# Who issues the DMAs: loads, rows of maxima and stores given to Sync, ScalarE or GpSimd by a new written order

## The chip, the cores and the metric

The kernel runs on one core of a Trainium2 chip. A core has five engines with a queue of instructions each: TensorE (PE, with its weight loads as PEld), VectorE (DVE), ScalarE (ACT), GpSimd (POOL) and Sync (SP). Each works through its own queue in order, and an instruction that waits holds all that stand behind it on that engine. The core's 16 DMA engines move data between memory and the on-chip buffer; a DMA is started by an instruction in the queue of Sync, ScalarE or GpSimd. The metric is the device time of the whole program in microseconds.

## What is computed

Two stages run one after the other: a linear attention with exponential features over 64 heads (8 batches of 8), 576 positions and 64 channels, and a feed-forward layer with a maximum of three products over its 4608 rows of 512.

```python
def phi(x):
    proj = np.einsum('bhsd,df->bhsf', x, w_phi)
    proj = proj - np.max(np.abs(proj), axis=-1, keepdims=True)
    return np.concatenate([np.exp(proj), np.exp(-proj)], axis=-1)
q_p, k_p = (phi(q), phi(k))
kv = np.einsum('bhsf,bhsd->bhfd', k_p, v)
z = np.sum(k_p, axis=2)
num = np.einsum('bhsf,bhfd->bhsd', q_p, kv)
den = np.einsum('bhsf,bhf->bhs', q_p, z)[..., None] + 1e-06
attn = num / den
...
x = np.ascontiguousarray(attn.transpose(0, 2, 1, 3)).reshape(B * S, H * D)
h = np.maximum(np.maximum(x @ w1, x @ w2), x @ w3)
out = h @ w_out
```

The inputs and the output are in float32; the products are made in bfloat16 with float32 sums.

## The kernel before

**Units and chunks.** The attention is cut into 16 units of four heads (two pairs), two units for each batch. A unit loads q, k and v as 128 rows of 18 tiles (576 KB each in float32), has them cast to bfloat16 (units 0 to 3: by the DMA or on ScalarE and VectorE; later ones on GpSimd, L480) and turned (units 0 to 3 on TensorE, L494 and L497; later ones by a transposing DMA from Sync, L512, into qkT). Then TensorE projects every tile (L535, in groups of four or two tiles, on halves of 64 rows), VectorE takes the largest absolute value of each row (L554) and ScalarE the two exponentials of k (L548). The maxima of q are turned on TensorE, copied out (L566, tile mT), and written by a small DMA, the "row of maxima", as one more row of qkT (L570), so that the product for q (L614) subtracts them; ScalarE then makes its exponentials (L627). The maxima of k become factors em (L585), by which GpSimd scales v (L589, tile vab, with a column of its own from L599). TensorE sums over the positions (L643, kvps), multiplies with q's exponentials (L661, psn), VectorE divides (L667, L668), and x is turned into xT (units 0 and 1 on TensorE, L681; later ones by a transposing DMA from Sync, L691).

The feed-forward layer works in 9 chunks of 512 positions, one for each batch, and a last one for the 64 remaining positions of all batches. A chunk makes six tiles of up-products in two rounds (L714, ups), evicted by ScalarE or VectorE (L722, L724: first round; L720: second round), then four tiles of output (L741 and L746, ops), evicted by ScalarE or VectorE (L754, tile osb, four buffers) and stored (L761, two DMAs for a tile; one in the last chunk, whose last tile is cut into three pieces). Weights are loaded by casting DMAs from GpSimd (L421); differences of them are made by six subtractions (L784, on VectorE or GpSimd; after one on VectorE, GpSimd makes a small copy at L787), and a product of the first table with w_out (L812, pm, evicted at L816) at the start.

**The written order.** Every piece of work is a Node with a table of costs, whose keys are the engines that it may run on, and a function that issues its instructions. The string PLAN (L96 to L245) lists all 1478 nodes in order. An entry is the node's number, a letter for its engine (T, D, A, G, S for TensorE, VectorE, ScalarE, GpSimd, Sync), a digit for the slot of each buffer that this node is the first to use, and the start that was planned for it. `plan` (L251) sets engine, start and slots from it; `fill` (L269) puts products with no use into gaps of TensorE's plan near the start (L843, `idler`, to keep its clock up), and issues all in the order of the planned starts. So the table fixes the order of each engine's queue, who does a piece of work that several engines may do, and which buffers are shared; the planned starts are not waited for. The nodes speak of "mode" for TensorE's use of 64 rows (1: L535 and L643; 2: L497) or of all 128 (0).

Loads come through L474 (the four first halves of unit 0 through L449; those of units 1 to 3 for q and k, which are cast on the way, from GpSimd through L463). A load needs its raw buffer free: there are two each for q and k, four for v. Three loads of v wait in addition for a tiny copy on VectorE (L472), which sets when they start. `queue_of` (L336) maps an engine's name to its queue; stores, rows of maxima and, after the change, loads use it.

Of the kernel before, what the change touches and what calls it, by code (L numbers as in the profile page):

```python
# [15 lines left out]
B, H, S, D = 8, 8, 576, 64  # L16
# [15 lines left out]
FULL = 1.45  # L32
# [64 lines left out]
0G@0.70 2D0@0.70 4A@0.70 10S0@0.70 3D@0.90 6S0@1.18 1G@1.25 8S@1.66 86G0@1.75 13S@2.14 85G@2.60 15S0@2.62 1076G@3.45 12A1@3.98  # L97
158G2@4.25 7D@4.96 159G@5.10 5D@5.46 16T1@5.61 9A@5.94 1079G@5.95 17D0@6.30 22T002300@7.08 27T45@7.30 26D@7.55 30D@8.15 14A@8.43
25D@8.76 23A@9.05 20T6@9.20 18T7@9.31 31D@9.37 21D@9.97 227G1@10.01 28A@10.12 19D@10.20 42T14@10.35 29A@10.62 45D@10.81
32T26@10.96 24A@11.11 46D@11.15 37T75@11.26 35D@11.49 34A@11.60 89T1@11.60 91T3@12.04 47A0@12.09 40D@12.10 44A@12.34 48G0@12.48  # L100
39A@12.68 90D1@12.71 61T20@12.86 33A@13.16 64T7@13.31 92D@13.33 228G@13.60 38A@13.65 36D@13.95 95T111311@14.10 66A@14.14
49G@14.45 41D@14.56 65A@14.63 43A@15.12 99D@15.16 110T67@15.27 63A@15.46 50G@15.57 55T5@15.61 98D@15.77 1077G@15.85 111A@15.94
1090T4@16.06 113D@16.38 62A@16.43 1088T1@16.66 56A@16.91 114D@16.98 67T2@17.26 97A@17.40 1086T6@17.49 1089D0@17.59 51A@17.89
69A@18.14 87D1@18.21 53G@18.29 58T0@18.34 1087D@18.34 88S@18.46 68A@18.48 57A@18.82 164T1@18.89 361S1@18.94 1091D@18.96
59A@19.30 93T2@19.34 52G@19.41 162T6@19.45 165D2@19.59 112A@19.79 166T5@19.90 163D@20.21 60A@20.28 105T41@20.36 54G@20.52
1078G@20.80 106A@20.83 108D@20.83 70T070@20.95 96A@21.32 160D2@21.44 167D@21.54 161S@21.69 94D@21.76 109D@21.98 100T64@22.05
296S0@22.17 115T53@22.27 101A@22.52 72D@22.59 362S1@22.65 1094T2@22.75 119D@22.96 102A@23.02 117A@23.50 104D@23.66 116A@23.84
1096T0@24.05 107A@24.18 103D@24.26 124A1@24.68 118D@24.87 120A@24.93 127G1@25.07 71A@25.18 1095D@25.21 183T003400@25.44
1097A@25.59 173T16@25.66 168T57@25.88 123A@26.09 177D@26.13 1098T2@26.23 185A@26.24 170A@26.73 186D@26.74 125G@27.00 175A@27.22
176D@27.35 137T01@27.52 184A@27.71 171D@27.95 77T30@27.98 126G@28.12 138A@28.23 1092T1@28.29 78D0@28.56 139A@28.71 172D@29.18  # L110
1099A@29.20 122G@29.23 79T5@29.58 174A@29.70 187D@29.79 75T3@29.90 1093A@30.18 140T0@30.21 121G@30.35 229D3@30.39 131T2@30.44
76D1@30.50 141A@30.69 73T6@30.89 142A@31.03 80D0@31.11 128T4@31.21 132A@31.37 11G@31.47 364G0@31.62 74D1@31.73 178T13@31.76
133A@31.85 143T105@31.98 130A@32.34 181D@32.35 129A@32.82 182D@32.96 188T26@33.08 233T1@33.31 145A@33.33 192D@33.57 144A@33.73
134T4@33.88 191D@33.91 196A0@34.13 234D0@34.25 146T51@34.34 190A@34.38 198G0@34.53 148T0@34.65 135A@34.72 147D0@34.90
235T2@35.06 231T1@35.17 189A@35.20 149D1@35.52 199A@35.55 136A@35.70 152T5@35.74 193T6@36.05 232D@36.14 179A@36.18 81T0@36.29
83T4@36.60 197G@36.62 169A@36.67 153D0@36.76 150T1@36.91 194A0@37.16 154T7@37.31 236D@37.38 180A@37.41 195S@37.56 151D1@37.60
242T115611@37.72 84A@37.90 247T23@38.05 155D@38.22 297S0@38.34 156T1@38.39 82D@38.69 230S@38.82 215T047@38.87 157A@38.95
1080D@39.16 426S1@39.30 249A@39.60 1081D@39.78 1104T0@40.09 244A@40.09 1082D@40.40 248A@40.58 1106T1@40.95 250D@41.02 216A@41.07
365G@41.37 251D@41.63 1102T4@41.81 1107A1@42.06 246D@42.23 1105A@42.56 366S1@42.64 1110T2@42.67 245D@42.84 243A@43.06
1084D@43.45 1108T3@43.54 1103A@43.55 1111A@44.05 1085D@44.07 252T10@44.50 217A@44.55 1083D@44.69 257T56@44.72 237T42@44.83  # L120
1109A@44.95 1112T7@45.17 240D@45.31 259A@45.45 299G2@45.66 239A@45.79 255D@45.91 1124T3@46.04 254A@46.28 1113D@46.52 253A@46.77
1422G@46.78 1116T4@46.90 260D@47.13 300G@47.18 238A@47.26 1125D@47.47 556S0@47.65 258A@47.75 209T10@47.76 262T7@47.98
1118T5@48.04 241D@48.09 263A1@48.29 429G1@48.30 211A@48.54 264S@48.69 261D@48.70 212T3@48.90 203T7@49.01 210A@49.02 1117D@49.04
1120T2@49.23 363S0@49.47 204A@49.51 1119D@49.66 427S1@49.95 205A@49.99 200T6@50.09 256D@50.28 1122T1@50.30 214A@50.48
1121D@50.89 265A1@51.04 206T4@51.17 213A@51.29 266G1@51.44 367T005700@51.48 1123D@51.51 202A@51.63 301S2@51.63 382T02@51.70
1114T3@52.04 201A@52.11 386D@52.17 370D@52.78 1130T1@52.91 384A@52.93 1115D@53.39 208A@53.42 267G@53.53 224T60@53.77 207A@53.91
371D@54.01 220T5@54.08 383A@54.39 275T31@54.40 1131T@54.61 385D@54.62 369A@54.88 225D0@55.22 368A@55.37 1101G@55.62 221D1@55.84
276A@55.86 222T4@55.90 491S1@56.07 218T2@56.22 1132A0@56.35 223D0@56.47 272T0@56.53 278T6@56.74 268G@56.82 273A@56.99
372T75@57.06 219D1@57.09 430G@57.10 284T114@57.28 277A@57.48 376D@57.70 226S@57.85 274A@57.96 375D@58.31 377T23@58.38 280A@58.45
1126T0@58.72 286D@58.92 279A@58.93 380D@59.30 373A@59.42 281T7@59.58 387T46@59.79 285D@59.91 282A@59.94 269T2@60.06 1127T@60.27  # L130
283A@60.28 381D@60.29 431S0@60.52 271A@60.62 391D@60.89 270A@61.11 390D@61.23 293T11@61.56 395A0@61.59 374A@61.84 291T7@61.87
396G0@61.99 294D0@62.12 289T4@62.19 379A@62.33 1134T2@62.50 290D1@62.75 1128A1@62.82 287T5@63.36 292D0@63.37 388A@63.43
1138T1@63.68 378A@63.77 288D1@63.99 397G@64.08 389A@64.26 317T114011@64.64 295S@64.76 302T73@64.86 312T65@65.08 319A@65.11
320D@65.11 1135T@65.42 313A@65.60 321D@65.75 303A@66.09 559G0@66.18 316D@66.35 304A@66.58 1139T@66.71 557S0@66.88 305D@66.96
1136A2@67.07 398G@67.30 298S1@67.36 306D@67.57 1100G@67.58 314A@67.68 392T4@68.00 307T72@68.16 318A@68.17 315D@68.17
414T053@68.38 308A@68.66 1140D3@68.78 309A@69.15 393D0@69.40 322T06@69.48 310D@69.60 1142T1@69.71 394S@69.75 323A@69.84
324A@70.18 311D@70.21 416A@70.52 622S1@70.53 1154T4@70.57 560G@70.68 325D@70.82 1143A0@70.92 1129S@71.01 326D@71.16 415A@71.42
1146T7@71.44 1155D@71.69 751S0@72.21 327T2@72.30 447T003000@72.45 328A1@72.61 432T16@72.68 1137S@72.69 442T54@72.90 448A@72.93
450D@72.93 1144T2@73.24 443A@73.42 445D@73.53 428S2@73.89 1147A@73.91 1152T3@74.10 451D@74.14 1141S@74.37 434A@74.41 1145D@74.75
444A@74.90 402T50@74.97 1148T7@75.18 435D@75.36 403A@75.43 818S3@75.57 330A1@75.92 411T2@76.05 329S@76.05 1150T1@76.16  # L140
404A@76.17 1149D@76.30 331G1@76.32 492S0@76.83 436D@76.91 1162T5@77.02 1151A@77.27 623S0@77.31 1153A@77.77 408T7@77.88
1156T1@78.10 1163D@78.13 412A@78.27 333G@78.41 413A@78.61 332G@78.69 446D@78.75 433A@78.95 1164T3@78.96 1157D@79.36 409A@79.44
405T5@79.82 449A@79.92 1158T2@80.04 1165D@80.07 406A@80.41 494G2@80.78 399T4@80.90 1160T6@81.12 1159D@81.15 401A@81.37
561S1@81.37 407A@81.85 437T10@82.08 1161D@82.23 349T132@82.30 400A@82.34 410A@82.82 441D@82.85 495G@83.27 452T54@83.40
1174T6@83.63 350A@83.65 455D@83.76 438A@84.05 351D@84.10 625G1@84.39 440D@84.48 340T71@84.49 439A@84.54 343T3@84.71 337T5@84.93
453A@85.03 334T2@85.14 421T00@85.36 344A@85.37 346T1@85.67 1175T@85.78 342A@85.85 422D0@85.92 496S2@86.20 336A@86.34 456D@86.54
345A@86.82 1166T0@87.07 348A@87.31 1176D1@87.32 347A@87.65 423T3@87.93 460A0@87.99 338A@88.24 419T6@88.25 462G0@88.39
424D1@88.50 417T1@88.56 335A@88.72 1167T@88.87 420D0@89.12 341A@89.21 339A@89.69 418D1@89.74 352T31@90.16 1168A2@90.41
354T2@90.47 754G0@90.48 425S@90.51 457T7@90.79 356T6@90.85 454A@91.02 355D0@91.04 358T5@91.16 458A0@91.36 577T111011@91.57
461G@91.60 353D1@91.66 572T47@91.79 1170T2@92.13 574A@92.26 359D0@92.28 579A@92.75 357D1@92.90 1171T@93.00 573A@93.24 575D@93.52  # L150
# [143 lines left out]
def kernel(  # L294
# [577 lines left out]
```

## Time and profile before

| what | value |
|---|---|
| median of 3 runs | 284.23 us (283.29 to 285.58) |
| profiled execution, span from first to last instruction | 282.5 us |
| 284.23 less the span | 1.7 us |
| busy share of PE, DVE, ACT, POOL | 96%, 75%, 68%, 40% |
| bytes read and written | 34.64 MB, 9.44 MB |
| granted clock of TensorE | 1.00 until the end |

The profile is taken from one execution. Its page gives only the span, no time of that execution measured from outside; the 1.7 us between span and median is what lies around it, start and last landing among them. In the views below, "SPq", "ACTq" and "POOLq" are the parts of an engine that wait and issue; a line such as "PE pm L812 <- DMA wout_bf: 1.0, 1, 1.0" tells who waited for whom, with the total in us, the number of waits and the longest. A row of groups gives line, engine, operation, output and input, the count, then busy us and mean ns, then the idle time just before and what ended it. In the view of the chain that ended last, a row is start, length and what it was.

### The profile page before, as it was taken

To read this page: it belongs to the slowest core of one execution; us is meant where nothing else is said; L and a number is where in the kernel's file an instruction comes from. 1 tells how busy PE (TensorE), PEld (TensorE's weight loads), DVE (VectorE), ACT (ScalarE), POOL (GpSimd) and SP (SyncE) were. 2 spreads that over 40 slices of the span, in tenths; PEclk is the share of its full clock that TensorE was granted. 3 is DMA by queue.
4 is the path that set the end of the run, shared out by engine and by line. 5 is a ranking of instruction groups with operands and counts; after the bars stand their busy time and mean duration, and the time that the engine had idled before them with its cause. 6 is when DMAs were issued, how large, how long until landed. Compare 5 with 4: busy or idle time off the path is not lost.

```text
span 282.5 us, 8556 instructions
## 1 busy us (share of the span) xinstructions
PE 271.2 (96%) x3521; PEld 154.0 (54%) x3560; DVE 211.6 (75%) x443; ACT 192.3 (68%) x449; POOL 113.2 (40%) x106
## 2 busy tenths in 40 slices
PE   8888979999999999999999999999999999999995
PEld 3565764566555644764556456555455465444443
DVE  4998989998877888679989876997477594254141
ACT  2897979898889779998585879977707961311111
POOL 8373567748176418913760563053033600000000
PEclk9999999999999999999999999999999999999999
DMA  7999999888999999999797866954975105600154
GB/s 202 240 206 282 280 273 240 266 204 167 300 363 198 175 308 300 194 165 277 212 199 129 246 235 124 166 102 167 186 177 116 40 4 104 137 2 0 37 123 139
DMA packets 68337, 51.45 MB, mean 182 GB/s; under 512 B 48778, under 2 KB 53066, under 8 KB 68298
## 3 DMA queue, kind: packets, MB, share of 16 engines
q1 hardware_dynamic: 63876, 45.74, 66.8%
q0 software_dynamic: 4000, 4.92, 10.0%
q8 instruction: 28, 0.46, 0.7%
q10 hardware_dynamic: 422, 0.24, 0.3%
q14 instruction: 11, 0.09, 0.1%
HBM read 34.64 MB, written 9.44 MB: 156 GB/s over the span
## 4 chain that ended last, share of the span: by engine, by line
PE 80%; DMA 11%; DVE 4%; issue 2%; SPq 1%; DVEq 0%
PE ups L714 31%; PE ops L746 14%; PE ops L741 10%; DMA wout_bf<-in_moe_w_out_dram 6%; PE psn L661 6%; PE kvps L643 5%; PE psm L614 5%; PE psq L535 4%; PE pm L812 2%; DMA out_dram<-osb 2%; DMA xT<-x_sb 2%; DVE x_sb L668 2%; DMA k_raw<-in_k_dram 1%; DVE mqp L554 1%; DVE mk L554 1%
## 5 line engine op out<-in xcount | busy, mean ns | idle before, releaser
L714 PE MATMUL ups<-xT,w_bf 128*128 128x512 bf16 x416 | 100.3, 379 | 1.4 <-DMA xT<-x_sb 0.3
L589 POOL TENSOR_TENSOR vab<-v_raw,em 128x1152 bf16<-128x1152 f32 (+1 forms) x36 | 68.2, 1907 | 67.2 <-ACT em L585 50.9
L548 ACT ACTIVATE Ek<-psk 128x512 bf16<-128x512 f32 (+1 forms) x160 | 80.8, 569 | 13.9 <-PE psk L535 10.1
L627 ACT ACTIVATE Eq<-psm 128x512 bf16<-128x512 f32 (+1 forms) x160 | 79.2, 570 | 7.3 <-PE psm L614 7.0
L714 PEld LDWEIGHTS <-w_bf 128*128 128x128 bf16 x432 | 41.0, 98 | 47.4 <-issue 0.4
L554 DVE TENSOR_REDUCE mqp<-psq 128x4 bf16<-128x512 f32 (+1 forms) x80 | 48.8, 631 | 6.3 <-PE psk L535 4.4
L746 PE MATMUL ops<-wout_bf,hT 128*128 128x512 bf16 (+2 forms) x215 | 49.3, 367 | 1.0 <-issue 0.5
L554 DVE TENSOR_REDUCE mk<-psk 128x4 f32<-128x512 f32 (+1 forms) x80 | 48.5, 628 | 2.4 <-PE psk L535 1.7
L720 DVE TENSOR_TENSOR hT<-hT,ups 128x512 bf16<-128x512 bf16 x54 | 36.1, 682 | 16.4 <-PE ups L714 12.7
L668 DVE TENSOR_TENSOR x_sb<-psn,rden 128x320 bf16<-128x320 f32 x64 | 31.5, 492 | 2.2
L746 PEld LDWEIGHTS <-hT 128*128 128x128 bf16 x228 | 21.1, 98 | 21.7
L722 ACT ACTIVATE hT<-ups 128x512 bf16<-128x512 f32 x33 | 19.1, 603 | 17.3 <-PE ups L714 15.8
L661 PEld LDWEIGHTS <-Eq 128*128 128x128 bf16 x640 | 25.0, 97 | 7.8 <-ACT Eq L627 0.2
L754 DVE COPY osb<-ops 128x512 f32<-128x512 f32 (+1 forms) x22 | 14.7, 669 | 16.8 <-PE ops L746 16.0
L661 PE MATMUL psn<-kv_sb,Eq 128*128 128x65 bf16 x640 | 26.9, 194 | 0.2 <-DVE mqp L554 0.2
L754 ACT COPY osb<-ops 128x512 f32<-128x512 f32 (+2 forms) x16 | 8.9, 562 | 23.2 <-PE ops L746 22.6
L741 PE MATMUL ops<-xT 128*128 128x512 bf16 x90 | 24.1, 380 | 0.3
L535 PE MATMUL psq<-w,qkT 64*128 64x128 bf16 x288 | 24.3, 217 | 0.1
L535 PE MATMUL psk<-w,qkT 64*128 64x128 bf16 x288 | 24.0, 217 | 0.4 <-ACT Eq L627 0.4
L535 PEld LDWEIGHTS <-qkT 64*128 64x128 bf16 x576 | 16.5, 94 | 12.0 <-issue 8.9
L614 PE MATMUL psm<-qkT,wphi_m 128*128 128x512 bf16 (+1 forms) x70 | 22.1, 358 | 0.0
L480 POOL CAST qk_bf<-q_raw 128x1152 bf16<-128x1152 f32 x12 | 13.8, 1147 | 20.3 <-DMA out_dram<-osb 9.4
(73 smaller groups left out, 230.9 us busy)
## 6 DMA issues: line engine op xcount, KB each, us to landing
v_raw<-in_v_dram SPq DMA_DIRECT2D x16, 576.0 KB
out_dram<-osb SPq DMA_DIRECT2D x64, 128.0 KB
q_raw<-in_q_dram SPq DMA_DIRECT2D x12, 576.0 KB
k_raw<-in_k_dram SPq DMA_DIRECT2D x12, 576.0 KB
w_bf<-in_moe_w_dram POOLq DMA_DIRECT2D x3, 768.0 KB, 20.3
qk_bf<-in_k_dram POOLq DMA_DIRECT2D x3, 288.0 KB, 13.9
qk_bf<-in_q_dram POOLq DMA_DIRECT2D x3, 288.0 KB, 13.4
wout_bf<-in_moe_w_out_dram POOLq DMA_DIRECT2D x1, 768.0 KB, 17.7
```

The source lines that it names most:

```text
L535: nc.tensor.matmul(ps()[:, i, :], lhsT=cols[r, :], rhs=w2[r, c, :], start=True, stop=True)
L548: nc.scalar.activation(Ek[s]()[:, tiles_of(t0, n), :], of(1), EXP, scale=1.0 - 2.0 * s)
L554: nc.vector.tensor_reduce((mq, mk)[c]()[:, tiles_of(t0, n)], of(c), AXX, ALU.max, apply_absolute_value=True)
L589: (nc.vector if n_.eng == "DVE" else nc.gpsimd).tensor_tensor(vab()[:, g, t0:t1, 0:D], vb()[:, t0:t1, :], em()[:, g, t0:t1].unsqueeze(2).t ...
L614: nc.tensor.matmul(psm()[:, 0:w], lhsT=wphi_m, rhs=rhs, start=True, stop=True)
L627: nc.scalar.activation(Eqb()[s][:, cols], psm()[:, 0:w], EXP, scale=1.0 - 2.0 * s)
L661: nc.tensor.matmul(psn()[:, c, :], lhsT=Eqb()[g][:, t0:t0 + P], rhs=kv()[:, pr, ab, g, :], start=(g == 0), stop=(g == 1))
L668: nc.vector.tensor_tensor(x_sb()[:, pr, :, ab, :], psn()[:, :, 0:D], rden().to_broadcast([P, 5, D]), ALU.mult)
L714: nc.tensor.matmul(ups(), lhsT=w_bf[i + 1][:, ct, j * P:(j + 1) * P], rhs=tokens_of(ct), start=(ct == 0), stop=(ct == CT - 1))
L720: nc.vector.tensor_tensor(hT()[:, j, :], hT()[:, j, :], ups(), ALU.max)
L741: nc.tensor.matmul(ops_()[:, 0:width], lhsT=tile_of(ct, tt), rhs=line_w[c_i > MOVE][:, ct, cols], start=(ct == 0), stop=False)
L746: nc.tensor.matmul(ops_()[:, 0:width], lhsT=hT()[:, j, tt * P:(tt + 1) * P], rhs=wout_bf[:, j, cols], start=False, stop=(j == JT - 1))
```

## The change

The edits of code are small: `queue_of` knows GpSimd; a load through L474 goes to the queue of its node's engine; and loads, rows of maxima and stores list the engines that may issue them. The table is new as a whole, 1478 entries again. It gives the same pieces of work another order on all engines, other slots, and for those that may run on several engines another choice. For the loads through L474 (40, all Sync's before) it names Sync 19 times, GpSimd 14 and ScalarE 7 times; for the 14 rows of maxima Sync 9, GpSimd 3 and ScalarE 2 times (before: Sync 12, ScalarE 2); for the 38 store steps Sync 20, GpSimd 14 and ScalarE 4 times (before: Sync 36, ScalarE 2). Of the six subtractions at L784 four go to GpSimd (before: all VectorE). Copies and evictions that VectorE, ScalarE or GpSimd may do also change sides in both directions.

```diff
-0G@0.70 2D0@0.70 4A@0.70 10S0@0.70 3D@0.90 6S0@1.18 1G@1.25 8S@1.66 86G0@1.75 13S@2.14 85G@2.60 15S0@2.62 1076G@3.45 12A1@3.98
...
+0G@0.72 6S0@0.73 2D0@0.85 3D@1.07 10S0@1.19 1G@1.29 4A@1.30 8S@1.65 85G0@1.79 13S@2.11 86G@2.64 1076G@3.49 7A1@3.63 15G0@4.29
+12D@4.68 158G2@5.14 16T1@5.33 9A@5.42 5D@5.85 159G@5.99 17D0@6.55 1079G@6.84 22T002300@7.32 27T45@7.56 25D@7.81 30D@8.41
...
-    queue_of = {"SP": nc.sync, "ACT": nc.scalar}
+    queue_of = {"SP": nc.sync, "ACT": nc.scalar, "POOL": nc.gpsimd}
...
-                mains.append(nd("Lv" if what == 2 else "L", {"SP": 0.62}, lambda what=what, raw=raw: nc.sync.dma_start(
-                    by_pairs(raw()), rows_of(what, u, 0, 2)), gates, [raw],
-                    pipe=(EARLY if u == 0 or u == BY_PE and what == 1 else 1.0) * FULL, hold=-3.0, lat=1.7,
-                    packet=PACKET))
+                def main(n_, what=what, raw=raw):
+                    queue_of[n_.eng].dma_start(by_pairs(raw()), rows_of(what, u, 0, 2))
+                n_ = nd("Lv" if what == 2 else "L", {"SP": 0.46, "ACT": 0.5, "POOL": 0.85}, None, gates, [raw],
+                        pipe=(EARLY if u == 0 or u == BY_PE and what == 1 else 1.0) * FULL, hold=-3.0, lat=1.7,
+                        packet=PACKET)
+                n_.fn = lambda n_=n_, f=main: f(n_)
+                mains.append(n_)
...
-            n_v = nd("V", {"ACT": 0.7, "SP": 0.7}, None, [n_mt] + projs, [mT, qkT], lat=2.2, pipe=0.1)
+            n_v = nd("V", {"ACT": 0.7, "SP": 0.7, "POOL": 0.9}, None, [n_mt] + projs, [mT, qkT], lat=2.2, pipe=0.1)
...
-                n_ = ff("store", {"SP": 0.6 * n_out, "ACT": 0.6 * n_out} if c_i == B else {"SP": 0.6 * n_out}, None, [e], [part],
+                n_ = ff("store", {"SP": 0.6 * n_out, "ACT": 0.6 * n_out, "POOL": 0.9 * n_out}, None, [e], [part],
```

Entry 15, for one, is the load of v of unit 0: 15S0 before, 15G0 after. In the changed file the lines behind L474 stand 3 lower.

More of the change, by code (lines that the diff above doesn't have):

```diff
@@ L101 @@
[L101 to L131, printed above, removed]
@@ L245 @@
+1465G@277.44 1474T5@277.83 1475T@278.05 1468A0@278.08 1469S@278.60 1476A2@278.63 1477A@278.90
 """
```

261 lines of the change are left out of this document (145 added, 116 removed).

## The prediction

> **What bounds the kernel now.** I read the page first, then the busy time by stages, then TensorE's own list of waits, and only then the list of the Sync queue, because the change is about issuing.
>
> ```profile
> span 282.5 us, 8556 instructions
> PE 271.2 (96%) x3521; PEld 154.0 (54%) x3560; DVE 211.6 (75%) x443; ACT 192.3 (68%) x449; POOL 113.2 (40%) x106
> ```
>
> ```profile
> 0.00:10.00 10.00, 8.43 (x54) 3.84 (x55) 5.78 (x19) 3.79 (x5) 5.87 (x13) 1.00 0.86 224
> 10.00:50.00 40.00, 36.33 (x719) 24.84 (x721) 36.87 (x80) 35.14 (x88) 24.26 (x30) 1.00 1.11 250
> 50.00:250.00 200.00, 197.34 (x2603) 111.05 (x2634) 158.29 (x330) 148.71 (x348) 83.03 (x64) 1.00 0.80 185
> ```
>
> The columns after the length are the busy time of TensorE (PE), its weight loads, VectorE, ScalarE and GpSimd, then the granted clock (1.00 throughout), the busy share of the DMA engines and GB/s. TensorE is the bound: between 50 and 250 us it is busy 197.34 of 200 us, so only 2.66 us are free there. Between 10 and 50 us 3.67 us are free, and in that stage the DMA engines are full (share 1.11). These 6.3 us are all that better issuing can give back. Next, who makes TensorE wait:
>
> ```profile
> PE pxT L681 <- issue: 1.3, 1, 1.3
> PE pm L812 <- DMA wout_bf<-in_moe_w_out_dram: 1.0, 1, 1.0
> PE ups L714 <- DMA xT<-x_sb: 0.3, 1, 0.3
> PE tps L497 <- DMA qk_bf<-in_q_dram: 0.3, 1, 0.3
> PE tps L497 <- DMA qk_bf<-in_k_dram: 0.3, 1, 0.3
> ```
>
> Waits that end with a transfer come to 1.0 + 0.3 + 0.3 + 0.3 = 1.9 us; one pause of 1.3 us has no releaser. The Sync queue tells another story:
>
> ```profile
> SPq L761 <- ACT osb L754: 21.3, 3, 19.3
> SPq L570 <- ACT Ek L548: 16.5, 3, 15.2
> SPq L474 <- DVE v_raw L472: 15.2, 1, 15.2
> SPq L761 <- DVE osb L754: 12.9, 9, 2.8
> ```
>
> Sync stands for tens of us behind evictions and gates, and the loads and transposes of the same queue stand behind it. But nearly none of it arrives at TensorE: the loads were issued early enough. That is the first reason for my forecast.
>
> **The change part by part.** Counted over both tables: of the 40 loads through L474 that Sync issued alone in the old table, the new one gives 14 to GpSimd and 7 to ScalarE; of the 14 rows of maxima 3 to GpSimd, and 2 are on ScalarE as before; of the 38 store steps 14 to GpSimd (12 of two DMAs, 2 of one, so 26 DMAs) and 4 to ScalarE (2 before). GpSimd gets 14 + 3 + 26 = 43 more DMAs. The same table also reorders every engine: four of the six subtractions of weight tables (L784) go from VectorE to GpSimd, and evictions change sides.
>
> *GpSimd's 43 DMAs.*
>
> ```profile
> L463 POOL DMA_DIRECT2D qk_bf<-in_k_dram x3 | 2.5, 817 | 0.0
> L463 POOL DMA_DIRECT2D qk_bf<-in_q_dram x3 | 2.2, 719 | 4.1 <-issue 4.1
> L421 POOL DMA_DIRECT2D w_bf<-in_moe_w_dram x3 | 2.4, 803 | 0.0
> L784 DVE TENSOR_TENSOR w_bf<-w_bf 128x1024 bf16<-128x1024 bf16 x6 | 3.8, 680 | 0.0
> L819 POOL COPY w_bf<-xT 128x1024 bf16<-128x1024 bf16 x2 | 2.1, 1042 | 0.0
> L589 POOL TENSOR_TENSOR vab<-v_raw,em 128x1152 bf16<-128x1152 f32 (+1 forms) x36 | 68.2, 1907 | 67.2 <-ACT em L585 50.9 <-DMA v_raw<-in_v_dram 13.7 <-issue 2.5
> L480 POOL CAST qk_bf<-k_raw 128x1152 bf16<-128x1152 f32 x12 | 13.7, 1148 | 13.8 <-DMA k_raw<-in_k_dram 13.8
> ...
> L589 POOL TENSOR_TENSOR vab<-v_raw,em x36: 1144/2123/2131, 12.4 to 223.6; 128x1152 bf16<-128x1152 f32 x28, 128x576 bf16<-128x576 f32 x8
> ...
> POOL vab L589 <- ACT em L585: 50.9, 11, 14.1
> ```
>
> A GpSimd issue keeps the engine for (2.5 + 2.2 + 2.4) / 9 = 0.79 us, whatever the size. A store or a row of maxima from GpSimd is not in the trace; between the 0.35 us of a store from ScalarE (below) and the 0.82 us here I take 0.79, the same engine. 43 x 0.79 = 34 us. A subtraction on GpSimd is not there either; it lies between the 1.04 us of a copy of that size and the 2.12 us of a full L589 product (its median), and I take the product: 4 x 2.1 = 8 us. GpSimd goes from 113 to about 155 us of 282. What hides it are its own waits, 67.2 us ahead of L589, of which 50.9 us in 11 waits for ScalarE's em (the last row: total, number, longest). The fullest stretch that I find in the new order is from about 96 to 124 us: 4 full products (8.5), 5 casts at 1.15 (5.7) and 9 DMAs (7.1) make 21.3 of 28 us. It fits, so I take 0. If the cover is gone, L589 is late, then the sums kvps (L643) on TensorE; that is a rival below, with +5.7 as the upper end.
>
> *Queues moved past.* Sync loses these issues, ScalarE gains 7 loads and two more store steps.
>
> ```profile
> L474 SPq DMA_DIRECT2D v_raw<-in_v_dram x16: 368/512/662, 2.6 to 205.2; - x16
> L761 SPq DMA_DIRECT2D out_dram<-osb x68: 332/587/1353, 72.7 to 279.7; - x68
> L761 ACTq DMA_DIRECT2D out_dram<-osb x2: 338/348/357, 278.0 to 279.2; - x2
> L570 ACTq DMA_DIRECT2D qkT<-mT x2: 717/1020/1324, 153.8 to 191.0; - x2
> ```
>
> The figures are shortest/median/longest in ns. Seven loads at the 0.51 us that Sync takes are 3.6 us of ScalarE, 68% busy before; queued behind each stand one or two exponentials (L548, L627), for which TensorE waits next. Bounds 0 (hidden) and +3.6 (all on the path); since ScalarE's busy time from 50 to 250 us leaves 51 us, I take 0. Sync's relief acts on the 2.66 us that TensorE is idle from 50 to 250 us. One such chain is visible:
>
> ```profile
> 97.94 5.07 DMA out_dram<-osb
> ...
> 103.10 0.69 DVE osb L754
> ...
> 107.43 1.02 PE ups L714 x4
> ```
>
> A store lands 5.07 us after its issue, in the middle of loads of the same queue; VectorE's next eviction waits for its buffer, and up-products follow. Bounds -2.7 (all of it goes) and 0; I take -0.6, less than a quarter, because most of the 2.66 us are short and spread, with no row above that names a transfer.
>
> *The start.* v of unit 0 goes from Sync to GpSimd's queue, ahead of two loads of unit 2 and of wout. Its 576 KB at the stage's 250 GB/s are 2.4 us: if they come ahead of wout, the 1.0 us wait of pm grows by up to +2.4; if the new order hides it and the 1.3 us pause, -2.3. The bytes that must land before wout are the same as before except for their queue, so I take 0 for the wait and half of the unexplained pause, -0.7.
>
> *TensorE's own order.* Projections (L535) and sums (L643) run on 64 rows, all else on 128. I counted the places where neighbouring steps of TensorE differ in that: 85 in the old table, 97 in the new.
>
> ```profile
> 43.90 2.37 PE ups L714 x11
> 46.27 0.16 PE psq L535
> 46.43 0.00 PE psk L535
> 46.44 0.05 PE psq L535
> ...
> 46.94 1.19 PE ups L714 x5
> ```
>
> Going in, the first product takes 0.16 instead of 0.05 us, 0.11 more; coming out, five up-products take 1.19 us where 2.37 / 11 x 5 = 1.08 would do, again 0.11. So 12 x 0.11 = +1.3 us; nothing hides it, as TensorE is the bound (0 if all fall into waits, the other bound). The Trainium skill, TensorEngine Tiling (Array Packing), Key Properties, says that a change of tiling mode drains the engine; it gives no price, and speaks against this order: by it the sum only grows. The rows above agree, with 0.11 us each.
>
> *The end.* The last eviction and store go to ScalarE (0.35 us, as above) instead of VectorE and Sync, and a piece before it is stored from GpSimd (0.79). Bounds -0.3 and +0.5; I take 0.
>
> **Sum** against the profiled execution: 282.5 + 0 (GpSimd) + 0 (ScalarE) - 0.6 (Sync's relief) - 0.7 (start) + 1.3 (changes of row form) + 0 (end) = 282.5 us. The median of the runs, 284.23, is 1.7 above that span; with the same 1.7 the forecast is 284.2 us: no change that can be measured (about 1% is what a measurement of this kernel can tell from none). Its own range, with the start's +2.4 and ScalarE's +0.9 for a quarter of its bound on one side and -2.0 of the gains on the other, is 282.2 to 287.5.
>
> **Rivals.** *A, faster.* The Sync waits above are what keeps TensorE from its last 4%: with three issuers half of the 6.3 idle us vanish (-3.2), and the 12 added changes of form fall into the rest (0). 282.5 - 3.2 = 279.3, so 281.0 us. For it: Sync's 21.3, 16.5 and 15.2 us. Against: only 1.9 us of TensorE's waits end with a transfer.
>
> *B, slower: GpSimd held by what it now issues.* A store waits for its eviction in the issuer's queue: on Sync (21.3 + 12.9) / 12 = 2.85 us each. In the new order seven stores and rows of maxima on GpSimd stand directly ahead of casts or products of a coming unit. The cushion there is on average 50.9 us of waiting for em, 4.6 us for each of its 11 waits; from the point where it is under 2.85 us, L589 is late by the difference, then kvps, and TensorE stops. If two of the seven are bare, 2 x 2.85 = +5.7: 288.2, so 289.9 us. Against it: the waits for em are long, and GpSimd is 76% busy in its fullest stretch (21.3 of 28).
>
> *C, slower issue on GpSimd.* VectorE could hold each new GpSimd issue for one of its instructions, 0.68 us (L784 above). In the stretch with 21.3 us, 9 x 0.68 = 6.1 more fill 27.4 of 28 us; the three rows of maxima come 0.68 later, and they have no cover: +2.0, so 286.2 us. The nine GpSimd issues above, at 0.72 to 0.82 us each on average, show no such hold. The Trainium skill, SBUF — State Buffer, Who interferes with whom, gives the rule for it: a VectorE instruction in a two-port mode locks GpSimd out while it would write descriptors, and a DMA from Sync or ScalarE is immune. Here most VectorE instructions read PSUM, so I give it little.
>
> *D.* The moved issues do what they say, but nothing hangs on them, and only TensorE's new order counts: +1.3 alone, 283.8, so 285.5 us. It is inside the forecast's own range and shares its chance.
>
> **How the numbers follow.** Forecast with D 0.54, A 0.22, B 0.18, C 0.06. A is the cases of faster by over 1%; B, and the upper edge of the forecast's own bounds, of slower; the forecast, D and C lie within 1% for nearly all. That makes faster 0.22, same 0.57, slower 0.21. The range reaches from a little below A's 281.0 to short of B's 289.9, and leaves out most of B's upper half and gains beyond A's: 280.6 to 289.0.
>
> **What would show it.** Right: TensorE's idle time from 50 to 250 us within 1 us of 2.66, its busy time up by about a us; GpSimd at about 155 us with issues of 0.7 to 0.9 us; Sync's waits for evictions mostly gone without effect. Start: pm (L812) begins within 1 us of where it did. Wrong: TensorE waiting for vab or for Ek for more than 2 us in all (B); GpSimd issues of 1.4 us (C); idle time from 10 to 250 us under 3.5 us (A); an end that lasts over a us longer after the last product.

## The result and the profile after

The changed kernel takes **301.58 us** (median of four runs, 299.08 to 304.09) where the kernel before takes 284.9 in the same set of runs (283.29 to 286.83). The ratio is 1.0559, with an interval of 1.0501 to 1.0618. The forecast was 284.2, with a range to 289.0: it missed by 17 us, and no rival had a time near it. Here and below, a median is taken over all executions, and a ratio with its interval over those within 1.5% of the fastest of their kernel; e4 and e9, with one such execution each, have no ratio.

The profiled execution took 300.46 us, with a span of 298.7. From its page, TensorE, the other engines and the row of the granted clock:

```profile
span 298.7 us, 8543 instructions
...
PE 278.4 (93%) x3520; PEld 155.5 (52%) x3561; DVE 211.2 (71%) x443; ACT 194.1 (65%) x449; POOL 144.4 (48%) x145
...
PEclk9999999999999999995999899999999999999999
```

The clock was even up to the end before. Here two slices, near 135 and 170 us, show half and four fifths of it. The same stages as in the prediction, with TensorE first and the clock in the third column from the end:

```profile
0.00:10.00 10.00, 8.78 (x55) 3.79 (x55) 5.47 (x20) 4.28 (x7) 6.64 (x14) 1.00 0.87 195
10.00:50.00 40.00, 37.17 (x708) 24.61 (x713) 36.24 (x78) 32.71 (x81) 29.38 (x30) 1.00 1.02 251
50.00:250.00 200.00, 188.79 (x2539) 106.20 (x2571) 155.54 (x324) 147.60 (x345) 104.75 (x95) 0.97 0.77 179
```

Up to 50 us TensorE idles 4.05 us (1.22 + 2.83) where it idled 5.24, 1.2 us less. Between 50 and 250 us it idles 11.21 us where it idled 2.66, and part of what it does there runs at half the clock. Its list of waits begins with a name that was not in the list of before at all:

```profile
PE psq L538 <- DMA qkT<-qk_bf: 6.3, 2, 4.1
PE kvps L646 <- POOL vab L592: 2.1, 2, 1.8
```

The projections wait for the transposing DMA that turns a unit's q and k. In the chain of work that ended last it stands twice (start, length, what):

```profile
124.08 11.98 DMA qkT<-qk_bf
...
158.93 9.88 DMA qkT<-qk_bf
```

Both end with the instruction that waited for them. They turn units 10 and 11. The landing events in the traces give the same for every transpose, waited for or not: before, units 10 and 11 landed 5.9 and 5.0 us after their issue, and none of the 12 transposes of this size took more than 8.7; here it is 12.0 and 9.9 us, and at most 8.2 for the other ten. (By the packets' own records the last packet came 4.1 to 7.4 us after the issue before; here 10.9 for unit 10, but only 7.1 for unit 11, whose landing event follows later.)

**Where the time is lost.** The written order makes this easy to read: the first product of each unit's sum (kvps) has a planned start in each table, and its lag behind the plan shows where the program falls back.

| sums of units, in order of time | before: planned, measured, lag | after: planned, measured, lag |
|---|---|---|
| 5th | 68.38, 70.06, 1.68 | 69.20, 71.29, 2.09 |
| 6th | 82.30, 83.97, 1.67 | 83.07, 87.55, **4.48** |
| 9th | 116.99, 119.00, 2.01 | 117.67, 122.32, 4.65 |
| 10th | 136.99, 139.24, 2.25 | 138.17, 149.87, **11.70** |
| 11th | 148.42, 150.47, 2.05 | 149.01, 160.67, 11.66 |
| 12th | 161.69, 163.72, 2.03 | 161.14, 176.60, **15.46** |
| 16th | 225.22, 227.24, 2.02 | 229.48, 244.99, 15.51 |

Three steps of 2.4, 7.0 and 3.8 us, 13.2 in all, and nothing in between. The two big ones are the two transposes: the 10th sum, of unit 9, stands in TensorE's queue behind the projections of unit 10, and the 12th, of unit 13, behind those of unit 11. This is the queue of Sync and GpSimd's issues at the first and at the second:

```profile
122.08 1.36 SPq L694 DMA_TRANSPOSE xT<-x_sb  x1
...
122.24 0.76 POOL L475 DMA_DIRECT2D k_raw<-in_k_dram  x1 [0.30 <-POOL qk_bf L483]
...
124.08 6.65 SPq L515 DMA_TRANSPOSE qkT<-qk_bf  x1
...
158.92 0.76 POOL L475 DMA_DIRECT2D k_raw<-in_k_dram  x1
...
158.93 3.31 SPq L515 DMA_TRANSPOSE qkT<-qk_bf  x1
```

Each time GpSimd issues a load of 576 KB within 2 us of a transpose. In the old order loads and transposes stood in one queue. There the issue for the same two units took 4.26 and 2.84 us:

```profile
120.29 4.26 SPq L512 DMA_TRANSPOSE qkT<-qk_bf  x1
...
147.80 2.84 SPq L512 DMA_TRANSPOSE qkT<-qk_bf  x1
```

A table of single microseconds of the changed kernel shows what the DMA engines do meanwhile (last three columns: granted clock, busy share of the DMA engines, GB/s):

```profile
122.00:123.00 1.00, 1.00 (x55) 0.92 (x56) 0.05 (x1) 1.00 (x4) 0.76 (x2) 1.00 0.00 0
...
124.00:125.00 1.00, 0.95 (x6) 0.47 (x5) 0.39 (x2) 0.95 (x3) 1.00 (x2) 1.00 1.87 36
...
132.00:133.00 1.00, 0.00 (x0) 0.00 (x0) 1.00 (x3) 0.26 (x1) 0.00 (x0) 1.00 1.36 40
...
135.00:136.00 1.00, 0.00 (x0) 0.00 (x0) 0.00 (x0) 0.00 (x0) 0.00 (x0) 0.62 0.94 314
136.00:137.00 1.00, 0.89 (x9) 0.47 (x10) 0.25 (x1) 0.16 (x1) 0.00 (x0) 0.50 1.11 328
```

At 124 and at 132 us the packets' records fill the DMA engines (1.87 and 1.36) and move 36 and 40 GB/s: they are in flight and do not get on. Such a microsecond is not new by itself; the kernel before has them too, without a wait on TensorE:

```profile
115.00:116.00 1.00, 0.95 (x5) 0.49 (x5) 0.54 (x2) 1.00 (x4) 1.00 (x1) 1.00 1.67 8
```

What tells the two kernels apart is the landing. From 132 to 136 TensorE does nothing, and from 135.2 on it has half its clock for 6.8 us. Behind the second transpose it stands still for 2.1 us, up to 168.85, and has half its clock for 3.4 us from 169.4 on.

### The profile page after: what moved, and what is told of

It is laid out like the page before. It is cut to its first block, busy times and chain, and to the rows that moved or that the text cites. A ratio compares the mean times of both kernels' runs of the same rounds, so it can differ in the third digit from the quotient of the medians.

```text
span 298.7 us, 8543 instructions
## 1 busy us (share of the span) xinstructions
PE 278.4 (93%) x3520; PEld 155.5 (52%) x3561; DVE 211.2 (71%) x443; ACT 194.1 (65%) x449; POOL 144.4 (48%) x145
## 4 chain that ended last, share of the span: by engine, by line
PE 66%; DMA 14%; POOL 8%; issue 5%; DVE 3%; ACT 2%; ACTq 0%; POOLq 0%
PE ups L717 29%; PE ops L749 11%; PE ops L744 8%; DMA qkT<-qk_bf 7%; PE psn L664 5%; POOL vab L592 4%; PE kvps L646 4%; PE psq L538 4%; PE psm L617 3%; DMA v_raw<-in_v_dram 3%; DMA qk_bf<-in_k_dram 3%; POOL qk_bf L483 2%; DMA xT<-x_sb 2%; ACT Ek L551 1%; DVE mk L557 1%
## 5 line engine op out<-in xcount | busy, mean ns | idle before, releaser
L551 ACT ACTIVATE Ek<-psk 128x512 bf16<-128x512 f32 (+1 forms) x160 | 81.7, 566 | 29.2 <-PE psk L538 25.6
L749 PE MATMUL ops<-wout_bf,hT 128*128 128x512 bf16 (+2 forms) x215 | 51.8, 379 | 1.3 <-issue 0.9
L764 POOL DMA_DIRECT2D out_dram<-osb x26 | 14.1, 547 | 48.2 <-ACT osb L757 39.4
L725 ACT ACTIVATE hT<-ups 128x512 bf16<-128x512 f32 x27 | 15.6, 597 | 31.3 <-PE ups L717 28.2
L538 PE MATMUL psq<-w,qkT 64*128 64x128 bf16 x288 | 25.5, 220 | 6.3 <-DMA qkT<-qk_bf 6.3
L664 PE MATMUL psn<-kv_sb,Eq 128*128 128x65 bf16 x640 | 28.2, 195 | 0.1
L757 ACT COPY osb<-ops 128x512 f32<-128x512 f32 (+2 forms) x24 | 13.4, 560 | 21.5 <-PE ops L749 18.7
L538 PEld LDWEIGHTS <-qkT 64*128 64x128 bf16 x576 | 16.8, 95 | 19.4 <-issue 9.8
L538 PE MATMUL psk<-w,qkT 64*128 64x128 bf16 x288 | 25.1, 219 | 0.3 <-DVE mqp L557 0.2
L727 DVE TENSOR_SCALAR hT<-ups 128x512 bf16<-128x512 f32 x27 | 18.4, 686 | 8.0 <-PE ups L717 7.8
L646 PE MATMUL kvps<-vab,Ek 64*128 64x65 bf16 x1152 | 20.6, 190 | 2.3 <-POOL vab L592 2.1
```

The costliest lines, as they stand in the source:

```text
L538: nc.tensor.matmul(ps()[:, i, :], lhsT=cols[r, :], rhs=w2[r, c, :], start=True, stop=True)
L551: nc.scalar.activation(Ek[s]()[:, tiles_of(t0, n), :], of(1), EXP, scale=1.0 - 2.0 * s)
L646: nc.tensor.matmul(kvps[ab]()[:, t // NT, g, :], lhsT=Ek[g]()[r, t, :], rhs=vab()[r, g, t, :], start=(t + g == 0), stop=(t == UT - 1 and g ...
L664: nc.tensor.matmul(psn()[:, c, :], lhsT=Eqb()[g][:, t0:t0 + P], rhs=kv()[:, pr, ab, g, :], start=(g == 0), stop=(g == 1))
L749: nc.tensor.matmul(ops_()[:, 0:width], lhsT=hT()[:, j, tt * P:(tt + 1) * P], rhs=wout_bf[:, j, cols], start=False, stop=(j == JT - 1))
```

## The experiments

Two theories stood at the start. **P**: GpSimd is held by what it now issues, stores and rows of maxima above all, so that vab and what hangs on it come late. **Q**: loads on a second or third queue run beside Sync's transposing DMAs and hold them up, TensorE stops at the projections, and its clock falls. Beside both stands the new order as such, with more changes of row form and its other end. Unless said otherwise, the edits stand in `plan`, ahead of the line that sets `n.end`, and act on the new table; later lines then stand two lower than in the changed kernel (L540 is its L538). The kernel before took 284.3 to 284.9 us in these sets.

### Taking issues back to Sync: e1, e2, e3

```diff
+        if n.kind in ("L", "Lv") and "SP" in n.costs:                    # e1
+        if n.kind in ("V", "store") and n.eng == "POOL":                 # e2
+        if n.kind in ("L", "Lv", "V", "store") and "SP" in n.costs:      # e3
+            n.eng = "SP"
```

> The new table with all 40 loads through L475 given back to Sync; rows of maxima and stores stay where the new table has them. Theory Q (loads from a second and third queue run amid Sync's transposing DMAs, which then land late; TensorE starves, and its granted clock halves after the starvation): the two long waits of the projections for qkT (4.1 and 2.2 us) and the half clock vanish, a transpose takes 4 to 6 us from issue to its last packet again, span about 286 (284 to 289). Theory P (GpSimd is held by what it issues, stores and rows of maxima above all): only the part of the loads goes, span 292 to 297. Theory O (the new order of the engines' work is worse by itself): 297 or more.

> The new table with GpSimd's 14 store steps and 3 rows of maxima given back to Sync; the loads stay on three queues. Theory Q: the waits for qkT stay, span 295 to 301. Theory P: the waits of GpSimd at the stores (some 48 us in all) and the late products at L592 go, span 285 to 290. Theory O: 297 or more.

> The new table, all loads, rows of maxima and stores on Sync, so that only the order of the work and the sides of evictions and subtractions are new. Theories Q and P: 283 to 287. Theory O: 297 or more. A value between says how much belongs to the order.

Measured: e1 298.14 us (ratio 1.0484, 1.0405 to 1.0562), e2 302.05 (1.0618, 1.0591 to 1.0646), e3 295.47 (1.0395, 1.0333 to 1.0457). **P falls with e2** as the main cause: GpSimd is rid of all its stores and rows of maxima, and nothing is gained in all; the wait for the transposes is even longer (units 10 and 11 land 11.0 and 13.8 us after their issue), and the end is 1.8 us shorter.

```profile
PE psq L540 <- DMA qkT<-qk_bf: 9.2, 2, 6.0
```

e1 and e3 gain little. By the numbers alone that speaks for the new order being worse by itself (theory O of the expectations), but the traces show another reason, and the middle no longer stalls. Two stages of e1:

```profile
0.00:50.00 50.00, 41.23 (x712) 26.62 (x714) 38.00 (x86) 31.60 (x74) 26.89 (x34) 0.94 0.96 229
50.00:250.00 200.00, 192.57 (x2592) 108.30 (x2628) 161.60 (x335) 152.96 (x357) 104.33 (x91) 1.00 0.75 182
```

From 50 us on the clock is whole and TensorE has 3.8 us more than in the changed kernel; but up to 50 us it idles 8.77 us instead of 4.05, at a clock of 0.94. The new order counts on three queues at the start: in one queue, loads and a row of maxima stand behind loads whose buffers are not free yet. The lag behind the plan says the same, and speaks against theory O: at the 5th sum e1 and e3 are 9.9 and 10.2 us behind (the changed kernel 2.1), and from there to the 16th they lose 5.2 and 4.0 us more, where the changed kernel loses 13.4. So the start had to be left alone.

### Only the later loads: e5, e6, e7, and GpSimd's small issues with them: e11

```diff
+        if n.kind in ("L", "Lv") and "SP" in n.costs and n.start > 60.0: # e5; e6: GpSimd's alone, to "ACT"
+            n.eng = "SP"
...
+        if int(what[:at]) in (947, 948, 817):                            # e7: k and v of unit 14, k of unit 12
+            n.eng = "SP"
...
+        if (n.kind in ("L", "Lv") and "SP" in n.costs and n.start > 60.0) or (n.kind in ("V", "store") and n.eng == "POOL" and "SP" in n.costs):   # e11
+            n.eng = "SP"
```

> The new table, but only the loads whose planned start is after 60 us (15 on GpSimd and ScalarE) go back to Sync; the start, the rows of maxima and the stores stay as the new table has them. Theory Q (a load of another queue that runs amid a transposing DMA makes the transpose land late): no transpose over 7 us from issue to last packet, no half clock in the middle, span 284 to 288. Theory P (GpSimd held by its stores and rows of maxima): 291 to 296. Theory O (order of work): 295 or more.

> The new table, with GpSimd's loads planned after 60 us moved to ScalarE's queue: no load waits in GpSimd or holds it, but they still share the DMA engines with Sync's transposes from another queue. Theory Q, any second queue does it: span 293 to 302, with transposes of 7 us and more. Theory Q in a narrow form, only GpSimd's queue does it: 284 to 289. Theory P: 288 to 294.

> The new table with three loads moved to Sync, those that ran beside the two slow transposes (k of units 14 and 12 from GpSimd, v of unit 14 from ScalarE). Theory Q: the two waits of 4.1 and 2.2 us and both stretches of half clock go, span 287 to 291, with the late sums of unit 4 (2.4 us) left. Theories P and O: 296 to 300.

> The new table, with the loads planned behind 60 us issued by Sync, as in e5 (289.4 us), and GpSimd's rows of maxima and stores issued by Sync too. If what is left of the loss in e5 is GpSimd's stores and the longer end (4.5 us from the last product on instead of 3.2): 285 to 288 us, the end 3 to 3.5 us. If it is the new order with its 12 more changes of row form: 288 to 291 us, TensorE busy about 274 us.

Measured: e5 289.38 us (1.0186, 1.0140 to 1.0231), e6 294.42 (1.0356, 1.0312 to 1.0401), e7 290.35 (1.0217, 1.0163 to 1.0272), e11 288.47 (1.0141, 1.0075 to 1.0207). **Three of the 40 loads**, back in Sync's queue, bring 11.2 of the 16.7 us by the medians (e7), or 3.4 of the 5.6% by the ratios. Its page and its list of waits:

```profile
PEclk9999999999999999999999999999999999999999
```

```profile
PE psq L540 <- DMA qkT<-qk_bf: 0.6, 1, 0.6
```

The lag of the 12th sum is 4.2 us there, instead of 15.5, and the issue of the first transpose takes 3.85 us instead of 6.65. The load of k goes out at nearly the same moment as before the move, 1.44 us ahead of that transpose instead of 1.84; the queue is what differs, and the transpose lands after 7.5 us instead of 12.0 (unit 11: 6.5 instead of 9.9):

```profile
122.44 1.31 SPq L477 DMA_DIRECT2D k_raw<-in_k_dram  x1
123.88 3.85 SPq L517 DMA_TRANSPOSE qkT<-qk_bf  x1
```

GpSimd's later loads on ScalarE's queue (e6) give back 7 us. The same two loads of k stand 1.40 us ahead and 0.07 us behind the same two transposes, which land after 9.1 and 8.7 us: less late than beside GpSimd's loads, later than beside Sync's own, so it isn't GpSimd as an engine alone. (e6's largest step lies elsewhere: its lag grows by 4.8 us at the 6th sum, with a wait of 1.2 us for ScalarE and 3.4 us of halved clock.) All later loads on Sync bring one more us than the three, GpSimd's stores and rows of maxima another 0.9; neither is clear of the spread of the runs (e5 288.64 to 290.43, e7 289.16 to 291.56, e11 287.04 to 290.89). e11 answers its two expectations half and half: the end shrinks to 2.9 us, but the time stays above 288 and TensorE is busy 275.0 us. What is left in e11 is 4.0 us.

### The old order with some of the new issuers: e4, e8

Both have the old table; e4 gives GpSimd and ScalarE the loads that the new table gives them, e8 gives GpSimd one of them, k of unit 12.

```diff
+        if int(what[:at]) in BY_POOL + BY_ACT:                           # e4: 14 and 7 loads, as in the new table
+            n.eng = "POOL" if int(what[:at]) in BY_POOL else "ACT"
...
+        if int(what[:at]) == 817:                                        # e8
+            n.eng = "POOL"
```

> The old table, with the loads alone given to the issuers of the new table (14 on GpSimd, 7 on ScalarE, the rest on Sync). Theory Q: several transposes land late, span 288 to 300. Theory P: loads hold GpSimd only where a buffer is not yet free, span 283 to 287. Theory O: 282 to 284.

> The old table, all on Sync as before but one load: k of unit 12 is issued by GpSimd. Theory Q: GpSimd has it out beside the transpose for unit 11, which then takes 10 us instead of 4 to 5; TensorE starves for some 4 us and runs at half clock for 3 to 7 us; span 287 to 291 where this happens, 283 in executions where the two miss each other. Theories P and O: 282 to 284.

e4 took 291.99 us, without the new order: 285.12 in one execution, 291.39 to 293.4 in the three others. In the profile, taken from the longest, one transpose (unit 11's) meets a load, 0.11 us apart, and in the chain it takes 13.23 us up to the instruction that waits for it:

```profile
149.92 2.62 SPq L521 DMA_TRANSPOSE qkT<-qk_bf  x1
...
150.03 0.75 POOL L481 DMA_DIRECT2D k_raw<-in_k_dram  x1
```

```profile
149.92 13.23 DMA qkT<-qk_bf
```

Whether the clash was missing in the execution of 285.12 us was not profiled; its granted clock, 0.999 instead of 0.988 to 0.994, fits that.

e8 took 284.65 us (1.0017, 0.9987 to 1.0048): a miss of the experiment. Alone, the load went out at 160.68 us, 12 us behind the transpose that it met in e4. That says only that such a load costs nothing when it meets no transpose.

### The clash made on purpose: e9, e10

The kernel before, with useless loads of k behind each transposing DMA of units 4 to 14, into a tile of their own and, up to unit 10, into one that is not yet in use.

```diff
             def tdma():
                 nc.sync.dma_start_transpose(...)
+                if u < UNITS - 1:
+                    nc.gpsimd.dma_start(dummy, rows_of(1, u, 0, 1)[:, 0, :])        # e10: nc.sync
+                if u < 11:
+                    nc.gpsimd.dma_start(x_last[1].rearrange("p c n -> p (c n)").bitcast(FP32), rows_of(1, u, 1, 2)[:, 0, 0:512])
```

> The kernel before, in its own order, with useless loads added: when Sync has issued a transposing DMA of qkT (units 4 to 14), GpSimd issues a load of 288 KB of k into a tile that nobody reads, and up to unit 10 a second one of 256 KB. No work is taken out. Theory Q (a load on another queue beside a transposing DMA holds it up): of the 11 transposes several take 6 to 12 us from issue to landing instead of 4.1 to 7.4, most of all those up to unit 10, TensorE waits 2 to 6 us at the projections behind them, the granted clock halves at least once, and the time is 290 to 305 us. If it is the new order or GpSimd's own time that costs (the 19 added issues are 19 x 0.75 = 14 us of an engine that idles for more than 100): transposes as before, 283 to 287 us.

> The same useless loads, issued by Sync itself behind each transposing DMA: the same bytes at nearly the same place, in one queue. Theory Q in its narrow form (two queues): Sync doesn't start the load before the transpose is through, transposes land within 4 to 7 us as before, and the time is 283 to 289 us, the later loads of Sync's queue being 2 to 3 us later each time. If it is the bytes beside the transpose, from whatever queue: as with GpSimd, 290 to 305 us.

e9 took 302.58 us (294.92 to 304.36), e10 290.62 (289.04 to 292.27; ratio 1.0222, 1.0148 to 1.0296). The order is the old one and the bytes are the same; **the edits differ in the queue alone, and it makes 12 us** by the medians (2.7 between e9's shortest and e10's longest execution). With the queue the moment changes too: Sync can issue its first useless load only when it is done with the transpose, 2.8 to 4.5 us behind its start, while GpSimd's first goes out between 1.9 us ahead and 3.5 us behind. In e9 five transposes land 10.6 to 18.1 us after their issue, in e10 none after more than 7.7. In e9 two in a row hold Sync for 18 us, and the wait that the changed kernel has is there:

```profile
89.30 17.97 SPq L513 DMA_TRANSPOSE qkT<-qk_bf  x2
```

```profile
PE psq L540 <- DMA qkT<-qk_bf: 9.8, 2, 7.9
```

The longer of the two waits, 7.9 us, ends with a landing; but e9 is not clean, since GpSimd also waits up to 6.9 us for its own earlier useless load. The stretch from 50 to 125 us, where both useless loads run, first in e9, then in e10:

```profile
50.00:125.00 75.00, 61.20 (x815) 34.30 (x824) 52.08 (x107) 51.08 (x120) 35.16 (x32) 0.93 1.12 232
```

```profile
50.00:125.00 75.00, 71.58 (x1060) 41.09 (x1071) 61.36 (x128) 63.77 (x152) 42.68 (x34) 1.00 1.04 275
```

The same bytes go through faster in one queue (275 GB/s instead of 232), with a lower busy share. In e10 no projection waits for a transpose. Its span is 5.1 us longer than before (287.6); 3.4 of them are longer waits for x, which lasted 0.3 us before:

```profile
PE ups L719 <- DMA xT<-x_sb: 3.7, 2, 1.8
```

The Trainium skill, DMA: Bandwidth & Descriptors, Issuing engines are not separate DMA queues, says that DMAs of several engines interleave on the same 16 DMA engines and that issuing them from several only saves the time of the issue; Rules for kernel authors, on the same page, says that a transpose next to ordinary DMAs needs nothing, in a row that is about wrong data. On the time the runs differ from the first rule: 302.58 us with a second queue, 290.62 with one.

### The same loads, later: e13

The three loads of e7 on their own queues, moved in the order.

```diff
+    for i, start in ((947, 124.0), (948, 157.0), (817, 152.0)):
+        nodes[i].start = start
+    order.sort(key=lambda n: n.start)
```

> The new table, with the three loads of e7 kept on their own queues (k of unit 14 and k of unit 12 by GpSimd, v of unit 14 by ScalarE) but put 5, 3 and 12 us later in the order, when the transposes of units 10, 7 and 11 should be through. If it is the moment (a load beside a transposing DMA): transposes of units 10 and 11 land within 6 us of their issue, no long wait for them on TensorE, and the time is 288 to 293 us, as e7's 290.35. If it is the second or third queue as such: 298 to 303 us, as the changed kernel.

e13 took 293.16 us (1.0253, 1.0154 to 1.0352): half of the loss is won back although no load changes its queue. With e8 it says that another queue does no harm by itself; with e7, where the moment stayed and the queue changed, that it takes both, another queue and the moment of a transpose. The transpose at 124.83 (unit 10) has no load issued within 3 us of it, its issue takes 3.13 us and it lands after 4.8. The move was not clean, though:

```profile
154.59 2.35 SPq L518 DMA_TRANSPOSE qkT<-qk_bf  x1
```

```profile
154.58 0.77 POOL L478 DMA_DIRECT2D k_raw<-in_k_dram  x1
```

Put 3 us later in the order, k of unit 12 still goes out 0.01 us from the transpose of unit 11, as in the changed kernel (158.92 and 158.93). And a load of v that ScalarE issued at 138.03 met the transpose of 137.18, which took 9.39 us in the chain. e13 stays 2.8 us above e7; these two are the visible reasons, not tried one by one.

### What the halved clock costs: e12, e14

The changed kernel with useless products on TensorE ahead of the two projections that wait, in `fill`.

```diff
+    for n, at, i in ((16, 127.149, 7), (9, 154.969, 2)):                # e12; e14: 9 and 5 instead of 16 and 9
+        todo += [(at, make(i)) for _ in range(n)]
     return [fn for _, fn in sorted(todo, key=lambda x: x[0])]
```

> The changed kernel with 25 useless products of 0.2 to 0.26 us added on TensorE ahead of the two projections that wait longest for a transpose (16 ahead of unit 10's, 9 ahead of unit 11's, in banks that are free there). No work is taken out. If the halved clock of 6.8 and 3.4 us behind these waits is the gate's answer to an idle TensorE, it goes, and half of 10.2 us with it: 296 to 298 us. If the clock is halved for another reason: 301 to 303 us, and the half clock stays at these places.

> As e12, but with 9 and 5 useless products instead of 16 and 9: in e12 one took 0.43 us from start to start, so that 16 lasted 6.9 us and ended 2 to 3 us behind the transpose's landing, and the halved clock that they avoided was paid back in products. With 3.9 and 2.2 us of them the transposes should still be the last thing that is waited for. If the halved clock has a price of its own (2 to 3 us here): 297 to 299.5 us, with less than 4 us of halved clock left. If it has none: 300.5 to 303 us.

e12 took 300.7 us (1.0568, 1.0510 to 1.0627). The clock was whole, 0.999, yet nothing was gained. My dose was wrong: a product took 0.43 us from start to start, and the last ended at 138.47, where the changed kernel's projections begin at 136.1.

```profile
131.67 0.34 PE idler L848
132.05 0.39 PE idler L848
132.48 0.39 PE idler L848
...
138.09 0.38 PE idler L848
```

With 9 and 5 of them (e14) the time is 297.56 us (1.0417, 1.0309 to 1.0526), **4 us less with 14 products more** (the two intervals overlap by a little, 1.0501 to 1.0526, so the size is not sharp). Its two runs with a granted clock of 1.00 took 295.65 and 295.95 us, those with 0.994 and 0.992 took 299.18 and 300.14. So the halved clock is most likely a loss of its own, about 4 of the 10.2 / 2 = 5.1 us that the records of the changed kernel suggest. The Trainium skill, TensorE: Matmul & The Clock Gate, What's actually happening, states a window of some 3.4 us of idleness that halves the clock; the traces agree in the steps, 3.4 and 6.8 us of halved clock, and it is gone where the waits were filled (e12); but here 2.1 us of standing still were enough for one of them. No threshold comes out of the runs: a stop of 1.2 us in e6 and one of 1.9 in e9 were followed by 3.4 us of halved clock too, stops of 1.8 us in e10 and 1.9 in e13 were not.

## Why the prediction was wrong, point by point

**The step that failed** is "Queues moved past" with its sentence on Sync's relief. I asked what transfers cost TensorE *now* (1.9 us of waits, 2.66 us idle in the long stage) and bounded the effect by 0 and a gain of 2.7. The other half of that question was missing: what a moved load does to the transfers that stay in Sync's queue. So the term -0.6 had no side on which it could cost time. Sync's queue kept loads and transposes apart, and that cover was gone with the change. The runs put 10 to 12 us in its place: e7 gets back 11.2 us by the medians (9.7 by the ratios) with three loads, e5 12.2 (10.6) with all later ones. The same gap let me write, at the start, that bytes are "the same as before except for their queue".

**GpSimd at 0**: right within the noise (e11 against e5: 0.9 us), for the reason given. Its busy time is 144.4 us, not 155, above all since a store takes 0.55 us and not the 0.79 that I took; the subtraction is as estimated:

```profile
L764 POOL DMA_DIRECT2D out_dram<-osb x26 | 14.1, 547 | 48.2 <-ACT osb L757 39.4 <-DVE osb L757 5.5 <-DVE rden L670 2.9
...
L787 POOL TENSOR_TENSOR w_bf<-w_bf 128x1024 bf16<-128x1024 bf16 x4 | 8.5, 2120 | 0.0
L475 POOL DMA_DIRECT2D v_raw<-in_v_dram x6 | 4.3, 726 | 3.0 <-DVE v_raw L472 3.0
```

Rival B is refuted by e2, although the 2.1 us that TensorE waits for vab crossed the mark that I had set for it: that wait ends with a load of v of unit 4 that landed late (GpSimd waits 6.83 us for it), not with a store. Rival C is refuted by the same rows: 0.55 to 0.76 us an issue, not 1.4. Rival A's gain did not come: TensorE idles more, not less.

**The start**: forecast -0.7, measured -1.2 in TensorE's idle time up to 50 us. The sign was right, the place mostly not: the wait of pm, for which I took 0, is gone (1.0 us), and the pause that I took half of fell from 1.3 to 0.8; pm itself begins at 24.1 instead of 23.4 us. The two runs with all loads on Sync (e1, e3) show that three queues are what the new start lives on.

**TensorE's own order**: the sign was right, the size too small. In e5, at full clock, TensorE is busy 274.1 us instead of 271.2, +2.9 where I took +1.3. Before, and then in e5, the rows that grow:

```profile
L661 PE MATMUL psn<-kv_sb,Eq 128*128 128x65 bf16 x640 | 26.9, 194 | 0.2 <-DVE mqp L554 0.2
L535 PE MATMUL psq<-w,qkT 64*128 64x128 bf16 x288 | 24.3, 217 | 0.1
...
L535 PE MATMUL psk<-w,qkT 64*128 64x128 bf16 x288 | 24.0, 217 | 0.4 <-ACT Eq L627 0.4
...
L497 PE MATMUL tps<-ident,qk_bf 128*64 128x128 bf16 x108 | 4.0, 221 | 0.6 <-DMA qk_bf<-in_q_dram 0.3 <-DMA qk_bf<-in_k_dram 0.3
```

```profile
L666 PE MATMUL psn<-kv_sb,Eq 128*128 128x65 bf16 x640 | 27.6, 194 | 0.1
L540 PE MATMUL psq<-w,qkT 64*128 64x128 bf16 x288 | 25.1, 218 | 0.9 <-DMA qkT<-qk_bf 0.8
L540 PE MATMUL psk<-w,qkT 64*128 64x128 bf16 x288 | 24.7, 218 | 0.3 <-DVE mqp L559 0.2
...
L502 PE MATMUL tps<-ident,qk_bf 128*64 128x128 bf16 x108 | 4.8, 223 | 0.9 <-DMA qk_bf<-in_k_dram 0.8
```

The same counts of products take 0.7 + 0.8 + 0.7 + 0.8 = 3.0 us longer, in the kinds that work on 64 rows and in short ones beside them; the mean of one hardly moves, so the time lies between neighbours. That it is the changes of form is argued from these rows, not tried by itself. The count of 12 is doubtful as well: it takes the products of L497 as a form of their own. Counted as the prediction words it, projections and sums against all else, the tables have 80 and 86 changes, six more; at 0.11 us each that leaves most of the 2.9 us unexplained.

**The end**: forecast 0, with +0.5 as the bound; measured +1.3 to +1.6, the sign of being wrong that the prediction names. From the end of the last product to the end of the span it is 3.2 us before, 4.8 after, 4.5 in e5, and 2.9 and 3.0 in e11 and e2, where the last stores of GpSimd go to Sync. The last lines of e5's order show that its last store by GpSimd is issued before the last eviction, and yet the end is later; I had counted its issue and not its landing.

```profile
281.90 0.55 POOL L766 DMA_DIRECT2D out_dram<-osb  x1 [1.75 <-DVE osb L759]
...
282.85 0.27 ACT L759 COPY osb<-ops 128x128 f32<-128x128 f32 x1 [0.19 <-PE ops L751]
...
283.14 0.34 ACTq L766 DMA_DIRECT2D out_dram<-osb  x1
```

**The sum again.** For e5: 282.5 + 2.9 (TensorE's rows) + 1.3 (end) + 0.6 (the rest, other idle time) = 287.3, its span. For the changed kernel 11.4 more, 298.7, with the late transposes and the halved clock behind them (e14: some 4 of them) as the cause. Open is the first step of the lag, 2.4 us at the 6th sum: a late load of v, with three loads issued by GpSimd and one by ScalarE within 3 us of one another. It is 0.7 in e5, where that load is Sync's, but also only 1.1 in e7, where it isn't; nothing tried it alone. Open is, too, what happens inside the DMA engines while packets are in flight and do not get on.

## What to carry to other kernels

A queue is also a fence: before a transfer is moved to another queue, list what it was kept apart from, and bound the loss of the transfers that stay, not only the gain of the engine that is relieved. In this kernel it paid to keep bulk loads in the queue of the transposing DMAs (e7), or to issue them where no transpose is due (e13); a load that the casting engine issues right behind its cast goes out with the transpose that this cast releases. And where TensorE starves, look at its granted clock as well: behind the stops of 2.1 and 4.1 us here it was halved for 3.4 and 6.8 us.

## What the hardware showed that I had not expected

- A transposing DMA of 576 KB beside a bulk load of another queue landed 8.2 to 13.2 us after its issue in the clashes of the changed kernel, e4 and e13, and up to 18.1 us in e9; with nothing beside it, 4.6 us (before, issues at 168.71 and 197.37 us).
- The same bytes behind the transpose in its own queue (e10): 275 GB/s from 50 to 125 us, and no landing after more than 7.7 us. A shared queue is no full cover: in e8, loads of Sync's own queue 2.7 and 2.3 us ahead of a transpose went with a landing after 9.3 us, which nothing waited for.
- The granted clock at half, for 3.4 or 6.8 us, behind standstills of 2.1 and 4.1 us; 14 useless products in the gaps made the program 4 us shorter.
- GpSimd issues a store in 0.55 us and a load in 0.72 to 0.76; ScalarE a load in 0.37 to 0.39.
